# Moving the S1, S2 and S3 visits of an FFT filter and maxout kernel to other steps

## The chip, the cores and the metric

The kernel runs on one core of a Trainium2 chip. The metric is the time of one execution in microseconds (us) on the device, the median of several runs. The profile is of one execution of its own.

## The reference

The input x has 8 batches of 3072 positions with 256 channels. Each batch is filtered in the frequency domain, and each token of the result goes through a maxout layer:

```python
X = np.fft.rfft(x, axis=1)
y = np.fft.irfft(X * (filt_r + 1j * filt_i)[None], n=3072, axis=1)
t = y.reshape(8 * 3072, 256)
out = np.maximum(t @ w1, t @ w2) @ w_out          # w1, w2: 256 x 1024, w_out: 1024 x 256
```

The kernel uses max(a, b) = b + relu(a - b): it multiplies by Wd = w1 - w2, clips at zero, multiplies by w_out, and adds t @ M with M = w2 @ w_out.

## The kernel before

**The filter.** The transform of length 3072 is split into 96 by 32, so that each piece is a matrix product. For one batch there are these pieces:

- `load_xf` (SyncE's DMA queue) and `fold` (GpSimd) bring in x in 8 chunks and form, for each chunk, the sum (line 103) and the difference (104) of the two halves of the sequence. The result is a tile xb.
- `s1(b, c)`, one for each chunk c of 0 to 7: four TensorE matmuls with CT into two PSUM tiles pa (line 349), two ScalarE evictions to at (353), and for odd c two DMAs to DRAM (ad). `s1_read` reads ad back, transposed, as bt.
- `s2(b, n)`, n of 0 to 5: eight matmuls of bt into two tiles px (376). `product` multiplies each px by the filter F on VectorE (382), giving pq.
- `s3(b, n)`: sixteen matmuls of pq into two tiles pz (399), two ScalarE evictions to zt (403), a DMA to DRAM (zd). `z_read` reads zd back as zr, in two halves.
- `s4(tt)`: eight matmuls of zr into two tiles py (428); one is evicted by ScalarE (432), one by VectorE (434). This gives y for a block tt of 384 tokens, eight blocks to a batch.

**The maxout layer.** `moe_h(tt, j)`, j of 0 to 7, multiplies y by 128 columns of Wd into a tile ph (448) and evicts it with relu to gt, on ScalarE (452) or on VectorE (450). From block 8 on, the steps with j of 1, 3 and 6 go to VectorE; before that, `on_v` lists them. `moe_o(tt, ...)` accumulates gt and y into a tile po (478, 480); each full po is copied to ot by VectorE (492), and `out_block` sends ot off by DMAs that GpSimd issues (461).

**The order.** All engines run their instructions in the order in which the program issues them, which is written out by hand. A batch b has 64 steps (step = 8 i + j, for block tt = 8 b + i). Each step issues `moe_h` of this block, then the visits planned for the step, then three or four matmuls of `moe_o` of the block before, then other planned work (`todo`: loads, folds, reads, t2). At j = 4 (at j = 6 in a batch's last block), s4 of the next block ends the step:

```python
for j in range(8):
    step = 8 * i + j
    if tt < 8 * B:
        moe_h(tt, j)
    for fn, a in mid.get((b, step), ()):       # visits
        fn(*a)
    ... # moe_o(tt - 1, ...)
    for fn, a in todo.get((b, step), ()):
        fn(*a)
    if j == (4 if i < 7 else 6) and tt + 1 < 8 * B:
        s4(tt + 1)
```

A visit works on the next batch and on the one after: `visit(b + 1, n, quads)` issues s3 of the visit before (n of 1 to 6), s2 of this one (n of 0 to 5), s1 of batch b + 2 for the chunks in `quads`, and the two products. Seven visits make a batch. `plan_f2(b, steps, quads, xs, folds)` gives their steps, the chunks of each, the steps of the loads (xs) and those of the folds. It also plans `z_read` three steps after the fourth and the seventh visit, and `s1_read` six steps after the last (eleven in batch 0). Batch 6 has no s1 left to do, and batch 7 has no visits.

**PSUM.** pa, px, pz, py, ph and a few others share one pool, `ps`, of six buffers; po has two buffers of its own. A new tile takes the buffer that has been free for longest in the program's order, and its first matmul waits for the eviction that frees it.

**The start.** Batch 0's filter runs by another path, with everything on chip: `t2(c, engines)` transposes chunk c of zT into PSUM (553) and copies it to zr, on VectorE (556), on ScalarE (558), or half on each. GpSimd forms Wd (292) and casts w2 (285) for `prep_t`, which transposes it (299).

Of the kernel before, what the change touches and what calls it, by code (L numbers as in the profile page):

```python
# [26 lines left out]
def kernel(  # L27
# [15 lines left out]
    V, S, G, TE = nc.vector, nc.scalar, nc.gpsimd, nc.tensor  # L43
# [621 lines left out]
    def plan(b, step, fn, *a):  # L665
        todo.setdefault((b + step // 64, step % 64), []).append((fn, a))

    def plan_f1(b, nb, steps, read):
        for c, n in zip(range(4, 16), steps):
            plan(b, n, f1, nb, c, S if c % 2 == 0 else V)  # L670
        plan(b, read, f1_read, nb)
# [3 lines left out]
    def plan_f2(b, steps, quads, xs, folds):  # L675
        for n, st in enumerate(steps):
            mid.setdefault((b, st), []).append((visit, (b + 1, n, quads[n])))
        plan(b, steps[3] + 3, z_read, b + 1, 0)
        plan(b, steps[6] + 3, z_read, b + 1, 1)
        if b + 2 < B:  # L680
            for c in range(8):
                plan(b, xs[c], load_xf, b + 2, c)
                plan(b, folds[c], fold, b + 2, c)
            plan(b, steps[-1] + (6 if b else 11), s1_read, b + 2)

    plan(0, 2, t2, 1, (V,))
    plan(0, 7, prep_t, 0)
    plan(0, 8, prep_t, 1)
    plan(0, 9, prep_m)
    for c in range(2, 8):  # L690
        plan(0, 8 * (c - 2) + (7 if c == 2 else 8), t2, c, (V,))
    plan_f1(0, 1, (5, 6, 7, 7, 10, 10, 11, 11, 12, 12, 13, 13), 14)
    plan_f2(0, (25, 28, 31, 35, 38, 42, 46), ((0,), (1,), (2,), (3,), (4,), (5,), (6, 7)),
            (8, 10, 15, 18, 21, 27, 30, 33), (16, 19, 25, 28, 31, 34, 38, 42))
    for b in range(1, B - 1):
        plan_f2(b, (7, 14, 18, 24, 31, 38, 42) if b > 1 else (14, 18, 24, 30, 34, 39, 42), ((0, 1), (2,), (3,), (4,), (5,), (6,), (7,)),
                range(-32, 32, 8) if b > 1 else range(-25, 31, 7), range(-22, 42, 8) if b > 1 else range(-15, 41, 7))

    for tt in range(8 * B + 1):
        b, i = divmod(tt, 8)  # L700
# [45 lines left out]
```

## Time and profile before

| | us |
|---|---|
| median of 3 runs (502.82 to 503.9) | 503.05 |
| profiled execution | 502.04 |
| its span, first to last instruction | 500.2 |
| TensorE busy | 488.7 (98%) |
| VectorE busy | 331.4 (66%) |
| ScalarE busy | 308.6 (62%) |
| GpSimd busy | 259.7 (52%) |

PE is TensorE's matmuls, PEld its weight loads, DVE VectorE, ACT ScalarE, POOL GpSimd, SP SyncE. The mean granted clock of TensorE is 0.992 of full speed. A line of the timeline gives the start, the length from first start to last end, the engine, the line of the kernel, the operation, its tiles and how many were merged. Matmuls are pipelined, so lines of TensorE overlap, and the time that one group takes is read from its start to the start of the next. Idle time of an engine and what ended it stand in brackets.

### The profile page before, as it was taken

What the parts mean: (1) busy time and instruction counts of PE and PEld (TensorE: products, weight loads), DVE (VectorE), ACT (ScalarE), POOL (GpSimd) and SP (SyncE); (2) the same over time, 40 slices, a digit from 0 to 9 for tenths busy, and PEclk for the clock granted to TensorE, in tenths of its full rate; (3) what the DMA queues carried; (4) which work ended last, traced back from release to release, by engine and by line L of the source; (5) the groups of instructions that cost most, each with busy time, mean ns of one, the idle gap of its engine ahead of it and who ended that gap; (6) DMA issues with size and microseconds to landing.
All of it is one profiled execution on the core that took longest, in us unless ns stands there. A gap on an engine that the chain in (4) does not pass through costs nothing.

```text
span 500.2 us, 13079 instructions
## 1 busy us (share of the span) xinstructions
PE 488.7 (98%) x5300; PEld 361.7 (72%) x5300; DVE 331.4 (66%) x514; ACT 308.6 (62%) x629; POOL 259.7 (52%) x342
## 2 busy tenths in 40 slices
PE   8699999999999999999999999999999999999996
PEld 4456767777777777777777777777777777777775
DVE  7786788458865786567755787457764687555552
ACT  6777478657764777557674677547774565544442
POOL 7894678548463954627654764637632221222220
PEclk9979999999999999999999999999999999999999
DMA  7999889996899668978789568896759236411112
GB/s 122 166 245 210 260 218 272 294 257 208 234 285 244 180 206 236 240 186 235 206 236 282 178 182 250 222 234 202 201 185 249 84 113 144 167 65 64 64 64 84
DMA packets 77981, 97.19 MB, mean 194 GB/s; under 512 B 8033, under 2 KB 54370, under 8 KB 77858
## 3 DMA queue, kind: packets, MB, share of 16 engines
q1 hardware_dynamic: 64658, 66.73, 51.4%
q0 software_dynamic: 13264, 29.64, 20.5%
q8 instruction: 41, 0.67, 0.6%
q14 instruction: 18, 0.15, 0.1%
HBM read 53.87 MB, written 47.19 MB: 202 GB/s over the span
## 4 chain that ended last, share of the span: by engine, by line
PE 93%; ACT 2%; DMA 1%; DVE 1%; POOL 1%; issue 0%; POOLq 0%
PE po L480 34%; PE ph L448 33%; PE po L478 8%; PE pz L399 5%; PE py L428 4%; PE pa L349 2%; PE px L376 2%; DMA xb<-in_x_dram 1%; PE pt L532 1%; PE pr L553 1%; PE pt L526 1%; PE pa L324 1%; ACT at L509 1%; DVE pq L382 0%; ACT bt L518 0%
## 5 line engine op out<-in xcount | busy, mean ns | idle before, releaser
L480 PE MATMUL po<-Wo,gt 128*128 128x256 bf16 x1536 | 261.0, 273 | 0.0
L452 ACT ACTIVATE gt<-ph 128x384 bf16<-128x384 f32 x321 | 157.2, 496 | 144.9 <-PE ph L448 144.2
L480 PEld LDWEIGHTS <-gt 128*128 128x128 bf16 x1536 | 146.6, 98 | 66.0 <-issue 10.3
L461 POOL DMA_DIRECT2D out_dram<-ot x186 | 103.0, 557 | 171.5 <-DVE ot L492 168.9
L450 DVE TENSOR_SCALAR gt<-ph 128x384 bf16<-128x384 f32 x191 | 105.0, 554 | 64.0 <-PE ph L448 62.0
L382 DVE TENSOR_TENSOR pq<-px,F 128x1024 bf16<-128x1024 f32 x91 | 107.0, 1220 | 23.3 <-PE px L376 22.7
L448 PEld LDWEIGHTS <-Wd 128*128 128x128 bf16 x1024 | 96.5, 98 | 12.1 <-issue 0.5
L103 POOL TENSOR_TENSOR xb<-XF 128x512 bf16<-128x512 f32 x48 | 61.3, 1276 | 53.1 <-PE py L428 24.3
L492 DVE COPY ot<-po 128x512 f32<-128x512 f32 x95 | 65.2, 686 | 25.1 <-PE po L480 24.0
L104 POOL TENSOR_TENSOR xb<-XF 128x512 bf16<-128x512 f32 x48 | 61.1, 1273 | 0.0
L353 ACT ACTIVATE at<-pa 128x512 bf16<-128x512 f32 x96 | 51.8, 608 | 2.4 <-PE pa L349 2.1
L403 ACT ACTIVATE zt<-pz 128x512 bf16<-128x512 f32 x84 | 45.6, 594 | 11.8 <-PE pz L399 9.7
L428 PE MATMUL py<-G,zr 96*128 96x96 bf16 x512 | 32.7, 206 | 0.4 <-DVE zr L556 0.3
L428 PEld LDWEIGHTS <-zr 96*128 96x128 bf16 x512 | 28.9, 97 | 3.0 <-DVE zr L556 1.0
L399 PE MATMUL pz<-pq,VP 64*64 64x256 bf16 x336 | 22.2, 281 | 0.1
L376 PE MATMUL px<-bt,U 64*64 64x256 bf16 x384 | 20.2, 277 | 1.2 <-ACT VQ L273 0.7
L399 PE MATMUL pz<-pq,VQ 64*64 64x256 bf16 x336 | 21.0, 269 | 0.0
L399 PEld LDWEIGHTS <-VP 64*64 64x64 bf16 x336 | 9.8, 105 | 13.6 <-issue 13.3
L349 PE MATMUL pa<-xb,CT 64*64 64x512 bf16 x192 | 19.5, 383 | 0.0
L376 PEld LDWEIGHTS <-U 64*64 64x64 bf16 x384 | 10.5, 108 | 4.1 <-issue 3.8
L563 PE MATMUL pd<-W 128*128 128x512 bf16 x28 | 10.2, 488 | 1.5 <-DVE zero L145 1.5
L349 PEld LDWEIGHTS <-CT 64*64 64x64 bf16 x192 | 8.7, 105 | 2.1 <-ACT gt L452 1.2
(429 smaller groups left out, 606.3 us busy)
## 6 DMA issues: line engine op xcount, KB each, us to landing
out_dram<-ot POOLq DMA_DIRECT2D x186, 128.0 KB, 3.5
XF<-in_x_dram SPq DMA_DIRECT2D x96, 192.0 KB, 5.1
ad<-at SPq DMA_DIRECT2D x56, 192.0 KB, 3.7
zd<-zt SPq DMA_DIRECT2D x42, 256.0 KB, 2.6
zr<-zd SPq DMA_DIRECT2D x56, 192.0 KB, 5.0
bt<-ad SPq DMA_DIRECT2D x13, 768.0 KB, 9.8
WS<-in_moe_w_dram SPq DMA_DIRECT2D x4, 512.0 KB, 7.1
xb<-in_x_dram POOLq DMA_DIRECT2D x8, 192.0 KB, 5.9
```

What stands on the lines that cost most here:

```text
L103: G.tensor_tensor(t_[:, 0], f[:, 0], f[:, 1], OP.add)
L104: G.tensor_tensor(t_[:, 1], f[:, 0], f[:, 1], OP.subtract)
L353: S.activation(at[:, m0:m0 + 2], pa[g], AF.Copy)
L382: E.tensor_tensor(pq, px.rearrange("p (o i) d -> p o i d", o=1).to_broadcast([128, 2, 2, D]), F[:, :, 2 * v:2 * v + 2, s], OP.mult)
L399: TE.matmul(pz[g][64 * s:64 * s + 64, i], tab[64 * g:64 * g + 64, 2 * v + i, s], pq[s][64 * g:64 * g + 64, q, i], start=(q == 0), stop=(q ...
L428: TE.matmul(py[:, m], zr[b][:, 4 * i + m, 128 * dc:128 * dc + 128], G1, start=True, stop=True)
L448: TE.matmul(ph, Wd[:, dc, 128 * j:128 * j + 128], y_[:, dc], start=(dc == 0), stop=(dc == 1))
L450: V.tensor_scalar(gt[tt][:, j], ph, 0.0, None, OP.max)
L452: S.activation(gt[tt][:, j], ph, AF.Relu)
L461: E.dma_start(out=dst, in_=ot[tt // 2][:, 3 * (tt % 2) + c])
L480: TE.matmul(p_, g_[:, n - 2, blk], Wo[:, n - 2], start=(e == 0), stop=(e == 9))
L492: V.tensor_copy(ot[tt // 2][:, e - 1:e + 1], po[q // 2 % 2])
```

## The change

Steps and chunks are planned anew; the work itself is the same, except that one t2 is split between two engines.

- t2 of chunk 1, at step 2 of batch 0, goes half to ScalarE and half to VectorE.
- Batch 0's second and third visits move from steps 28 and 31 to 29 and 32.
- In batches 1 to 5 the first visit has one s1 chunk instead of two, and the last has two instead of one.
- In batches 2 to 6 the visits move from steps 7, 14, 18, 24, 31, 38, 42 to 7, 12, 18, 23, 28, 34, 39; in batch 1 from 14, 18, 24, 30, 34, 39, 42 to 14, 18, 23, 28, 34, 39, 42. The steps of loads and folds stay, those of `z_read` and `s1_read` move with the visits.

```diff
-    plan(0, 2, t2, 1, (V,))
+    plan(0, 2, t2, 1, (S, V))
...
-    plan_f2(0, (25, 28, 31, 35, 38, 42, 46), ((0,), (1,), (2,), (3,), (4,), (5,), (6, 7)),
+    plan_f2(0, (25, 29, 32, 35, 38, 42, 46), ((0,), (1,), (2,), (3,), (4,), (5,), (6, 7)),
             (8, 10, 15, 18, 21, 27, 30, 33), (16, 19, 25, 28, 31, 34, 38, 42))
     for b in range(1, B - 1):
-        plan_f2(b, (7, 14, 18, 24, 31, 38, 42) if b > 1 else (14, 18, 24, 30, 34, 39, 42), ((0, 1), (2,), (3,), (4,), (5,), (6,), (7,)),
+        plan_f2(b, (7, 12, 18, 23, 28, 34, 39) if b > 1 else (14, 18, 23, 28, 34, 39, 42),
+                ((0,), (1,), (2,), (3,), (4,), (5,), (6, 7)),
                 range(-32, 32, 8) if b > 1 else range(-25, 31, 7), range(-22, 42, 8) if b > 1 else range(-15, 41, 7))
```

## The prediction

> **What bounds the kernel now.** I read the page first. TensorE carries the chain, with almost nothing between its instructions.
>
> ```profile
> PE 488.7 (98%) x5300; PEld 361.7 (72%) x5300; DVE 331.4 (66%) x514; ACT 308.6 (62%) x629; POOL 259.7 (52%) x342
> PE 93%; ACT 2%; DMA 1%; DVE 1%; POOL 1%; issue 0%; POOLq 0%
> ```
>
> Then I cut the span into batches (table of windows: us, then busy us of each engine): TensorE is busy for the whole of a steady batch, so a moved visit costs or gains only what it makes TensorE wait.
>
> ```profile
> 222.49:279.90 57.41, 57.41 (x612) 42.92 (x608) 38.37 (x56) 37.06 (x77) 34.27 (x42) 1.00 0.81 221
> ```
>
> The page's waits are too coarse for this, so I read TensorE's timeline from start to start. A step is .65 to .76 us, or 1.10 with an s4. A visit adds 1.09: .09 for the turn to 64-row tiles, s3 .46, s2 .22, one s1 .32. A second s1 in the same visit adds .22 (the first line below, the last visit of batch 0, has 86.72 to 87.26 = .54 for two). Whatever exceeds that is waiting. The third line is a clean s4: py to the next ph in .34.
>
> ```profile
> 86.72 0.60 PE L349 MATMUL pa<-xb,CT 64*64 64x512 bf16 x8
> 222.32 0.81 PE L349 MATMUL pa<-xb,CT 64*64 64x512 bf16 x8
> 227.10 0.51 PE L428 MATMUL py<-G,zr 96*128 96x96 bf16 x8
> 227.44 0.49 PE L448 MATMUL ph<-y__4206,Wd 128*128 128x384 bf16 x2
> ```
>
> **What the change removes.** The pa of a visit's last s1 takes the PSUM buffer of the same step's ph, so it waits for that ph's eviction. An eviction on VectorE takes 558 ns against ScalarE's 491, and the pa comes at about the moment when the latter ends.
> - Batches 2 to 5: step 7 has .75 for its two s1 (222.32 to 223.07) against .54: .21. Steps 14 and 38 (VectorE): .38 against .32 each: .06. Step 24, the first of a token block, whose ScalarE eviction has one more semaphore to pass: .05. New steps 7 (one s1 and no s3, so no buffer of its own step), 12, 18, 23, 28, 34, 39 are all ScalarE steps: 0, as at 18 and 31 now. Gain .38 a batch, 1.54 in four.
> - Batch 1: step 14 .28 (.82 for two s1), 24 .05, 30 .06: .39. Batch 6 has no s1: nothing.
> - Batch 0: step 28 runs from 64.20 to 67.32, 3.12 us, and step 29 ends at 68.08. Moved: step 28 in 1.10, step 29 with the visit 1.86 (as 132.22 to 134.08), and .06, since its ph is on VectorE: end at 67.22. Gain .86; step 32, where the next visit now shares VectorE with t2, may give .1 of it back, or none.
> - t2 split over ScalarE and VectorE: py waits for zr until 40.10. The halves have rows (.59 on ScalarE, .42 on VectorE, in t2 of chunk 0), so zr is ready some .28 earlier. But step 7's pt starts at 41.91 behind GpSimd's cast of w2b, whose first half ends at 41.85 and does not depend on py. I take 0; the ends are -.28 and +.1 (ScalarE's next evictions .1 late).
>
> **What it adds at steps 12 and 28.** There j = 4, and an s4 follows in the same step. In the built order py takes the two buffers that zt0 and zt1 release, and the next ph the one that at0 releases: three evictions in a row on ScalarE. Batch 0's step 28 is such a visit today (first five lines TensorE, then ScalarE):
>
> ```profile
> 65.39 0.48 PE L376 MATMUL px<-bt,U 64*64 64x256 bf16 x8
> 65.61 0.48 PE L349 MATMUL pa<-xb,CT 64*64 64x512 bf16 x4
> 66.03 0.61 PE L480 MATMUL po<-Wo,gt 128*128 128x256 bf16 x4
> 66.47 0.69 PE L428 MATMUL py<-G,zr 96*128 96x96 bf16 x8
> 67.32 0.48 PE L448 MATMUL ph<-y__1318,Wd 128*128 128x384 bf16 x2 [0.16 <-ACT at L353]
> 65.70 1.08 ACT L403 ACTIVATE zt<-pz 128x512 bf16<-128x512 f32 x2 [0.48 <-PE pz L399]
> 66.67 1.09 ACT L353 ACTIVATE at<-pa 128x512 bf16<-128x512 f32 x2
> ```
>
> py to ph is .85 instead of .34: .51 lost. ScalarE was idle before zt, so nothing of its load explains it; at0 ends 1.57 after zt begins, while TensorE would want the buffer 1.1 after that. In a steady visit zt begins .21 after px (229.30 against 229.09), at0 ends 1.79 after px, ph starts at 1.84, and the clean sum is .22 + .32 + .44 + .34 = 1.31: .52 again. Bounds 0 and .61 (with the .10 that this pa waited); I take .52. Visits with an s1 at such a step: one in batch 1 (28), two in each of batches 2 to 5, so 9 x .52 = 4.7. In batch 6, without s1, ph takes zt0's buffer, free by then: 0. Queued behind: y on ScalarE and VectorE, needed four steps later; no cost.
>
> **What it adds at step 39.** The s1 of chunk 7 moves there from step 42, while its fold stays planned at step 34, and a visit now stands at step 34. Its two products go into VectorE's queue ahead of that step's copy of ot, the two output DMAs on GpSimd wait for the copy, and the fold stands behind them in GpSimd's queue. Today batches 2 to 5 have no visit at 34: step 34 starts at 248.10, the second half of the fold ends at 253.46, 5.36 later, and s1 comes at 256.36. Batch 1 has the visit at 34 today and shows the new order (step 34 starts at 132.22; VectorE, then GpSimd):
>
> ```profile
> 133.53 2.36 DVE L382 TENSOR_TENSOR pq<-px,F 128x1024 bf16<-128x1024 f32 x2 [0.93 <-PE px L376]
> 135.80 0.68 DVE L492 COPY ot<-po 128x512 f32<-128x512 f32 x1
> 136.78 1.09 POOL L461 DMA_DIRECT2D out_dram<-ot  x2 [6.65 <-DVE ot L492]
> 137.89 1.28 POOL L103 TENSOR_TENSOR xb<-XF 128x512 bf16<-128x512 f32 x1
> 139.12 1.29 POOL L104 TENSOR_TENSOR xb<-XF 128x512 bf16<-128x512 f32 x1
> 137.36 0.49 PE L448 MATMUL ph<-y__2587,Wd 128*128 128x384 bf16 x2
> ```
>
> The fold ends at 140.41, 8.19 after step 34 began. The last line is step 39, 5.14 after step 34. In the changed visit the second s1 comes .88 (ph, s3) and .22 (first s1) later: 6.24. TensorE, in order, waits until about 8.24: 2.0 in each of batches 2 to 5, 8.0 together. Bounds 0 (the fold as early as today, 5.36) and 2.3 (GpSimd a slot later). I take 2.0, since every term is a row of the same order. Batch 1 keeps its chunk 7 at step 42, where the fold ends 1.15 before (140.41 against 141.55): no wait.
>
> The DMAs that move along: z_read of batches 2 to 5 from steps 27 and 45 to 31 and 42, s1_read from 48 to 45, on SyncE past loads of x at other steps. Four z_read issues hold SyncE 1.98 us in batch 0; the loads behind them feed folds that are used 5 to 20 us later; 0, or a few tenths if I am wrong.
>
> **Sum**, against the profiled execution (502.04; its span 500.2): -1.54 - .39 - .86 + 4.7 + 8.0 = +9.9, so 511.9. The median of the runs is 503.05, 1.01 above the profiled one: 513.0.
>
> **Rivals.**
> - Fold in time: the copy of ot or the fold comes as early as today, and only s4 loses. For it: VectorE has idle time around. Against it: the built order has both products before the copy, as batch 1 has. +1.9: 505.0. Chance .07.
> - No s4 loss, but the fold waits: if py and ph found other buffers. Against it: the built order names zt0, zt1, at0. +5.2: 508.3. Chance .06.
> - Faster: a visit's backlog delays nothing behind it. ScalarE's four evictions (2.17 us) and VectorE's two products (2.36 us) would have to clear at the pace of the steps without a visit; it decides at .5 us (at0 before 1.31 after px) and at 2.0 us (fold). Then only the gains are left, -2.8: 500.3. The one sight of each order speaks against it. Chance .05.
> - The clock falls. From 20.9 to 24.3 TensorE was busy for 1.14 of 3.4 us, and in the next 6.8 us the granted clock was half:
>
> ```profile
> 20.90:24.30 3.40, 1.14 (x40) 0.66 (x40) 2.85 (x4) 2.74 (x6) 3.33 (x4) 0.99 0.73 133
> 24.30:31.10 6.80, 6.21 (x132) 3.14 (x131) 6.65 (x6) 4.73 (x11) 6.80 (x4) 0.50 0.97 250
> ```
>
>   A wait of 2.0 us, with one pa inside it, leaves some 1.6 busy of 3.4; from 17.5 to 20.9 it was 2.51 and the clock stayed full. So the case lies between the two. Each spell would cost 6.8 x .5 = 3.4: 516.4 with one, 526.6 with four. Chance .10. The Trainium skill ("TensorE: Matmul & The Clock Gate", Part 1: The HAM clock gate) asks for an idle window of about 3.4 us before the clock is halved. By that rule, which the row above does not bear out in full (a third of its window was busy), no spell comes, and the sum stays.
>
> **Numbers.** The forecast has .72. Its own range is 510 to 514.5. For 8 in 10 I reach from the 508.3 case to one spell of the slow clock: 508.0 to 517.0, which leaves out 500.3, 505.0 and several spells. A measurement here tells about 0.2% (1 us) from no change. Faster .05 (backlog rival), same .02 (a share of the fold rival in which s4 loses less), slower .93.
>
> **What would show it.** Right: four waits of TensorE at pa behind L103 and L104, each about 2 us in all, once per batch 2 to 5, with the fold ending some 8.2 after step 34; py to ph at .86 in nine visits; single pa at .32 and step 7 without a wait; pt still at 41.9. Wrong: no wait of TensorE on GpSimd; steady batches near 57.4; or a granted clock under 1.00 behind the waits.

## The result, and the profile after

The changed kernel takes 513.95 us (median of 6 runs, 513.49 to 515.13), the one before 502.94 (6 runs, 502.19 to 503.9): a ratio of 1.0223, 95% interval 1.0206 to 1.0239. The forecast was 513.0. The profiled execution took 513.72 with a span of 511.7, against 502.04 and 500.2: 11.5 us more span.

The page first: TensorE is 2.5 us busier in a span that is 11.5 longer (the same matmuls: part of a matmul's wait is counted as busy, 58.22 us in a steady batch against 57.41), and its share of the chain has fallen from 93% to 84%, with DMA, ScalarE and GpSimd on the chain.

```profile
PE 491.2 (96%) x5300; PEld 362.0 (71%) x5300; DVE 329.2 (64%) x514; ACT 308.8 (60%) x630; POOL 259.9 (51%) x342
PE 84%; DMA 5%; ACT 4%; POOL 4%; DVE 1%; issue 1%; POOLq 0%
```

The table of windows, from the start of a batch to the start of the next (batches 2 and 3, then batch 1, then batch 6): us, then TensorE's busy time. A steady batch takes 60.03 instead of 57.41, and no longer all of it is busy. Batch 1 takes 57.97; in the trace of before, its window 101.24 to 158.69 has 57.45. Batch 6, without s1, takes 55.29 as before (55.30).

```profile
159.84:219.87 60.03, 58.22 (x611) 43.17 (x608) 38.03 (x57) 37.12 (x77) 33.12 (x40) 1.00 0.81 217
219.87:279.90 60.03, 58.22 (x610) 43.16 (x608) 38.03 (x57) 37.13 (x77) 33.09 (x40) 1.00 0.77 212
101.87:159.84 57.97, 57.78 (x611) 42.99 (x608) 38.15 (x57) 36.92 (x77) 32.53 (x39) 1.00 0.91 243
399.97:455.26 55.29, 55.29 (x579) 41.54 (x576) 38.02 (x57) 29.55 (x61) 13.10 (x25) 1.00 0.36 116
```

So batches 2 to 5 cost 4 x 2.62 = 10.5 and batch 1 .52. What is left, .5, lies at the two ends: batch 1 starts .63 later (101.87 against 101.24), and what follows the last batch's matmuls is .15 shorter. The waits of TensorE alone (us in total, times, longest) name the new causes; of these five, the trace of before has only the third, once (.2 us, at batch 0's step 28):

```profile
PE pa L349 <- POOL xb L104: 3.4, 4, 0.8
PE pa L349 <- POOL xb L103: 2.4, 4, 0.6
PE ph L448 <- ACT at L353: 1.4, 9, 0.2
PE po L480 <- DMA Wo<-in_moe_w_out_dram: 0.8, 1, 0.8
PE ph L448 <- DVE pq L382: 0.6, 1, 0.6
```

The idle times are shorter than what is lost, because the modelled end of the matmul before covers the first part of each wait. From start to start the loss is whole. Step 39 of batch 3, on TensorE:

```profile
257.50 0.49 PE L448 MATMUL ph<-y__4679,Wd 128*128 128x384 bf16 x2
258.38 0.39 PE L349 MATMUL pa<-xb,CT 64*64 64x512 bf16 x4
259.35 0.37 PE L349 MATMUL pa<-xb,CT 64*64 64x512 bf16 x1 [0.59 <-POOL xb L103]
260.57 0.41 PE L349 MATMUL pa<-xb,CT 64*64 64x512 bf16 x3 [0.84 <-POOL xb L104]
260.91 0.50 PE L480 MATMUL po<-Wo,gt 128*128 128x256 bf16 x3
```

The two s1 take 258.38 to 260.91 = 2.53 instead of .54: 1.99 lost. VectorE and GpSimd show why, in the order that batch 1 had shown before: the visit's products, the copy of ot, the two output DMAs, the fold.

```profile
253.67 2.36 DVE L382 TENSOR_TENSOR pq<-px,F 128x1024 bf16<-128x1024 f32 x2 [0.93 <-PE px L376]
255.94 0.68 DVE L492 COPY ot<-po 128x512 f32<-128x512 f32 x1
256.92 1.09 POOL L461 DMA_DIRECT2D out_dram<-ot  x2 [4.83 <-DVE ot L492]
258.02 1.28 POOL L103 TENSOR_TENSOR xb<-XF 128x512 bf16<-128x512 f32 x1
259.24 1.27 POOL L104 TENSOR_TENSOR xb<-XF 128x512 bf16<-128x512 f32 x1
```

Step 34 starts at 252.35, so the fold ends 8.16 after it. And step 28 of batch 3, with s4 behind the visit (TensorE, then ScalarE): py to ph is 248.66 - 247.80 = .86 instead of .34, while pa takes a clean .31.

```profile
247.04 0.39 PE L349 MATMUL pa<-xb,CT 64*64 64x512 bf16 x4
247.80 0.70 PE L428 MATMUL py<-G,zr 96*128 96x96 bf16 x8
248.66 0.32 PE L448 MATMUL ph<-y__4498,Wd 128*128 128x384 bf16 x1 [0.16 <-ACT at L353]
247.03 1.09 ACT L403 ACTIVATE zt<-pz 128x512 bf16<-128x512 f32 x2
248.00 1.09 ACT L353 ACTIVATE at<-pa 128x512 bf16<-128x512 f32 x2
```

### The profile page after: what moved, and what is told of

The parts are those of the page before. It is cut to its first block, busy times and chain, and to the rows that moved or that the text cites. A ratio compares the mean times of both kernels' runs of the same rounds, so it can differ in the third digit from the quotient of the medians.

```text
span 511.7 us, 13077 instructions
## 1 busy us (share of the span) xinstructions
PE 491.2 (96%) x5300; PEld 362.0 (71%) x5300; DVE 329.2 (64%) x514; ACT 308.8 (60%) x630; POOL 259.9 (51%) x342
## 4 chain that ended last, share of the span: by engine, by line
PE 84%; DMA 5%; ACT 4%; POOL 4%; DVE 1%; issue 1%; POOLq 0%
PE po L480 31%; PE ph L448 31%; PE po L478 8%; PE pz L399 4%; PE py L428 3%; DMA Wo<-in_moe_w_out_dram 2%; ACT zt L403 2%; PE px L376 2%; PE pa L349 2%; DMA xb<-in_x_dram 1%; DMA zd<-zt 1%; DVE pq L382 1%; POOL xb L103 1%; POOL xb L104 1%; ACT at L353 1%
## 5 line engine op out<-in xcount | busy, mean ns | idle before, releaser
L480 PE MATMUL po<-Wo,gt 128*128 128x256 bf16 x1536 | 261.1, 273 | 0.8 <-DMA Wo<-in_moe_w_out_dram 0.8
L480 PEld LDWEIGHTS <-gt 128*128 128x128 bf16 x1536 | 146.2, 98 | 67.5 <-issue 12.4
L450 DVE TENSOR_SCALAR gt<-ph 128x384 bf16<-128x384 f32 x191 | 104.5, 553 | 70.9 <-PE ph L448 59.3
L492 DVE COPY ot<-po 128x512 f32<-128x512 f32 x95 | 65.2, 686 | 37.9 <-PE po L480 35.0
L428 PE MATMUL py<-G,zr 96*128 96x96 bf16 x512 | 34.1, 205 | 0.4
L349 PE MATMUL pa<-xb,CT 64*64 64x512 bf16 x192 | 20.4, 378 | 5.7 <-POOL xb L104 3.4
L349 PEld LDWEIGHTS <-CT 64*64 64x64 bf16 x192 | 8.7, 105 | 8.7 <-issue 4.4
## 6 DMA issues: line engine op xcount, KB each, us to landing
bt<-ad SPq DMA_DIRECT2D x13, 768.0 KB, 10.5
```

The lines of the kernel that those rows point to most:

```text
L428: TE.matmul(py[:, m], zr[b][:, 4 * i + m, 128 * dc:128 * dc + 128], G1, start=True, stop=True)
L450: V.tensor_scalar(gt[tt][:, j], ph, 0.0, None, OP.max)
L480: TE.matmul(p_, g_[:, n - 2, blk], Wo[:, n - 2], start=(e == 0), stop=(e == 9))
L492: V.tensor_copy(ot[tt // 2][:, e - 1:e + 1], po[q // 2 % 2])
```

## The experiments

The theory: two losses that have nothing to do with each other, the fold of chunk 7 behind step 34's visit (8.0) and s4 behind a visit (9 x .52), against gains of some 2. The rivals: the fold is late for its load, steps at j = 4 are dear by themselves, or the two s1 of the last visit are. The runs were made on three chips, and each is compared with the kernel before on its own chip, where that took 502.93 or 503.79 us. In the cuts of code, ... stands for what is left out of a line.

**The fold a step earlier.**

```diff
-    ... range(-22, 42, 8) if b > 1 else range(-15, 41, 7))
+    ... (-22, -14, -6, 2, 10, 18, 26, 33) if b > 1 else range(-15, 41, 7))
```

> The changed kernel with the fold of chunk 7 planned at step 33 instead of 34 in batches 2 to 6, so that GpSimd has it ahead of the output DMAs that wait for step 34's copy of ot. Theory (the fold stands in GpSimd's queue behind a copy that stands behind the visit's two products): the wait of 1.99 us at step 39 goes in all four batches, 513.95 - 4 x 1.99 = 506.0, and the s4 losses of .515 stay. Rival (the load of x or SyncE's order makes the fold late): the fold ends as late as before, 513.5 to 514.5. Rival (the clock or the rest gives part back): between.

506.54 us, 1.0060 of the kernel before (1.0037 to 1.0083), where the changed kernel had 1.0223. The fold now ends at 253.65, 3.8 us before the visit's s1 begins, ahead of the outputs in GpSimd's queue, and the two s1 of step 39 take .54:

```profile
252.38 1.27 POOL L104 TENSOR_TENSOR xb<-XF 128x512 bf16<-128x512 f32 x1
255.99 1.12 POOL L461 DMA_DIRECT2D out_dram<-ot  x2 [2.33 <-DVE ot L492]
257.44 0.60 PE L349 MATMUL pa<-xb,CT 64*64 64x512 bf16 x8
257.98 0.50 PE L480 MATMUL po<-Wo,gt 128*128 128x256 bf16 x3
```

The load was there in time, then; the place in the queue was the cause. The nine losses at py stay at .515 each.

**The user of the fold a visit later.**

```diff
-    ... (7, 12, 18, 23, 28, 34, 39) if b > 1 else (14, 18, 23, 28, 34, 39, 42), ...
+    ... (7, 12, 18, 23, 28, 34, 42) if b > 1 else (14, 18, 23, 28, 34, 39, 42), ...
```

> The changed kernel with the last visit of batches 2 to 6 at step 42 instead of 39; the fold of chunk 7 stays at step 34, behind the visit of that step. Theory: the fold ends as late as in the changed kernel, about 8.2 after step 34 begins, but s1 of chunk 7 comes about 2.2 later and finds it done or nearly done: -8.0 + 0 to .4, 506.0 to 506.5. Rival (two s1 in the last visit, not the fold, make the wait): it stays, 513 to 514.

506.42 us, 1.0072 (1.0053 to 1.0091). Step 34 starts at 250.26 and the fold ends as late as in the changed kernel, but the last visit's two s1, from 258.46 on, need no wait:

```profile
255.92 1.28 POOL L103 TENSOR_TENSOR xb<-XF 128x512 bf16<-128x512 f32 x1
257.15 1.27 POOL L104 TENSOR_TENSOR xb<-XF 128x512 bf16<-128x512 f32 x1
258.46 0.60 PE L349 MATMUL pa<-xb,CT 64*64 64x512 bf16 x8
```

So a late fold costs nothing by itself, and two s1 in one visit do not make the wait either. They are not quite free: py to ph takes .42 instead of .34 at step 44 of these four batches, as in the run with the chunks alone below.

**The visits off the steps with s4.**

```diff
-    ... (7, 12, 18, 23, 28, 34, 39) if b > 1 else (14, 18, 23, 28, 34, 39, 42), ...
+    ... (7, 13, 18, 23, 29, 34, 39) if b > 1 else (14, 18, 23, 29, 34, 39, 42), ...
```

> The changed kernel with the visits of steps 12 and 28 one step later, at 13 and 29 (j = 5, also a ScalarE step), ahead of which s4 has been issued. Theory (py and the next ph wait for the zt and at evictions of the visit just before): nine times .515 go, 513.95 - 4.6 = 509.3, the waits at step 39 stay. Rival (ScalarE is simply too full around j = 4 and 5, wherever the visit stands): most of the .515 stays and shows up at the next ph or pa, 513 to 514.

510.01 us, 1.0119 (1.0095 to 1.0144). In its trace all nine py are clean, and the visits at 13 and 29 have no wait. The waits at step 39 are 1.99 to 2.00, as before.

**One such visit on the kernel before.**

```diff
-    ... (7, 14, 18, 24, 31, 38, 42) if b > 1 else (14, 18, 24, 30, 34, 39, 42), ...
+    ... (7, 12, 18, 24, 31, 38, 42) if b > 1 else (14, 18, 24, 30, 34, 39, 42), ...
```

> The kernel before with one edit: the second visit of batches 2 to 6 at step 12 instead of 14. Step 12 is a ScalarE step with an s4 behind the visit. Theory: in each of batches 2 to 5 it loses .515 at py and the next ph and gains the .06 that step 14 waits now, so 4 x .455 = +1.8: 504.8 against 502.94; batch 6 shows neither. Rival (the change's own idea, a ScalarE step is better): 4 x -.06, 502.7.

505.19 us against 502.93: 1.0049 (1.0030 to 1.0068), 1.5 to 3.4 us more, with 1.8 expected. Step 12 loses .515 in batches 2 to 5 and nothing in batch 6. Its lines in batch 3: .86 from py to ph.

```profile
229.07 0.70 PE L428 MATMUL py<-G,zr 96*128 96x96 bf16 x8
229.93 0.48 PE L448 MATMUL ph<-y__4206,Wd 128*128 128x384 bf16 x2 [0.16 <-ACT at L353]
```

**s4 a step later, the visits left.**

```diff
-            if j == (4 if i < 7 else 6) and tt + 1 < 8 * B:
+            if j == (5 if i < 7 else 6) and tt + 1 < 8 * B:
```

> The changed kernel with s4 issued at the end of the step j = 5 instead of j = 4 in all blocks but a batch's last; the visits stay at 12 and 28. Theory (buffers): between visit and s4 one step of .76 us passes, so that the evictions are over, and py takes buffers that are free: 9 x .515 less, 509.3. Rival (a visit at j = 4 is dear by itself): 513 to 514.

512.27 us, 1.0171 (1.0151 to 1.0192): 1.7 us less than the changed kernel, where 4.6 were expected. The loss at py is gone (172.38 to 172.72 is a clean .34), so the nearness of visit and s4 is what costs. A new wait has come three steps on: the first ph of the next block needs VectorE's half of y, and that eviction now stands behind the visit's products and a copy of ot. In batch 2 (TensorE, then VectorE):

```profile
172.38 0.51 PE L428 MATMUL py<-G,zr 96*128 96x96 bf16 x8
172.72 0.49 PE L448 MATMUL ph<-y__3214,Wd 128*128 128x384 bf16 x2
174.14 0.72 PE L448 MATMUL ph<-y__3375,Wd 128*128 128x384 bf16 x2
171.07 2.36 DVE L382 TENSOR_TENSOR pq<-px,F 128x1024 bf16<-128x1024 f32 x2 [0.81 <-PE px L376]
173.34 0.68 DVE L492 COPY ot<-po 128x512 f32<-128x512 f32 x1
173.94 0.55 DVE L434 TENSOR_SCALAR y__3375<-py 128x384 bf16<-128x384 f32 x1
```

y ends at 174.49 and ph, begun at 174.14, takes .56 instead of .33. The loss is .24 in the nine visits that had .515, and .45 in the two of batch 6, which had none, so the trace gains 9 x .28 - .9 = 1.6 in batches 1 to 6. The expectation had looked at buffers alone.

**Both repairs.** The fold at step 33 and the visits at 13 and 29.

```diff
-    ... (7, 12, 18, 23, 28, 34, 39) if b > 1 else (14, 18, 23, 28, 34, 39, 42), ...
+    ... (7, 13, 18, 23, 29, 34, 39) if b > 1 else (14, 18, 23, 29, 34, 39, 42), ...
-    ... range(-22, 42, 8) if b > 1 else range(-15, 41, 7))
+    ... (-22, -14, -6, 2, 10, 18, 26, 33) if b > 1 else range(-15, 41, 7))
```

> Both edits on the changed kernel: fold of chunk 7 at step 33, visits at 13 and 29. Theory: the two losses are separate, so both go, 513.95 - 8.0 - 4.6 = 501.3, that is 1.6 below the kernel before. Rival (one of them hides part of the other): 502 to 504.

500.99 us against 503.79 on the same chip: .9949 (.9932 to .9966), faster than the kernel before by 1.7 to 3.4 us. A steady batch takes 57.06 and TensorE is busy for all of it:

```profile
212.85:269.91 57.06, 57.06 (x610) 42.88 (x608) 38.01 (x57) 37.33 (x76) 33.10 (x40) 1.00 0.78 222
```

57.41 - 57.06 = .35 is the gain of the change's own idea, which the two losses had covered; .38 a batch had been forecast, and step 39 now loses .05 at po.

**Batch 0's visits alone, on the kernel before.**

```diff
-    plan_f2(0, (25, 28, 31, 35, 38, 42, 46), ...
+    plan_f2(0, (25, 29, 32, 35, 38, 42, 46), ...
```

> The kernel before with batch 0's second and third visits at steps 29 and 32. The prediction's step: -.86, 502.1. What the changed kernel's trace suggests: of that, .2 goes at pa of step 29 and .74 at step 42, where the next ph has got the buffer of px and waits for VectorE's product: net -.1 to +.1, 502.9. If the wait at step 42 isn't there, it was not of this edit.

503.06 us against 502.93, ratio 1.0011 (.9988 to 1.0034): no gain. The pa of step 29 loses .20, and behind the visit of step 42 the next ph starts .74 late: in the built order it has px's buffer, and product 0 (VectorE, second line) frees that only at 84.4.

```profile
83.54 0.38 PE L478 MATMUL po<-M,y__1441 128*128 128x256 bf16 x2
83.21 2.35 DVE L382 TENSOR_TENSOR pq<-px,F 128x1024 bf16<-128x1024 f32 x2 [0.47 <-PE px L376]
84.48 0.48 PE L448 MATMUL ph<-y__1683,Wd 128*128 128x384 bf16 x2 [0.56 <-DVE pq L382]
```

**And the three later visits a step on.** Steps 38, 42 and 46 become 39, 43 and 47; the expectation calls them two.

```diff
-    plan_f2(0, (25, 28, 31, 35, 38, 42, 46), ...
+    plan_f2(0, (25, 29, 32, 35, 39, 43, 47), ...
```

> The kernel before with batch 0's visits at 25, 29, 32, 35, 39, 43, 47: as the second and third visit alone, but the two later ones a step on, where the built order gives the ph behind the sixth visit the buffer of zt, not that of px. Theory: the .74 wait is gone, and of the .86 some .6 are left: 502.3. Rival (the wait comes from late DMAs of zt): it stays, 502.9.

502.37 us, .9984 (.9961 to 1.0007): the time can't tell. In the trace the .74 is gone (.05 at each of the three visits moved on); the .20 at step 29 stays, and .13 at step 32.

**The chunks alone, on the kernel before.**

```diff
-    ... ((0, 1), (2,), (3,), (4,), (5,), (6,), (7,)),
+    ... ((0,), (1,), (2,), (3,), (4,), (5,), (6, 7)),
```

> The kernel before with only the chunks moved: the first visit of batches 1 to 5 has one s1, the last (step 42) two. Theory: step 7's wait of .21 goes in four batches and step 14's .28 in batch 1, but in batch 1 the second s1 of step 42 waits for the VectorE eviction of step 41 behind step 39's products (.40, as in the changed kernel): -.84 - .28 + .40 = -.72, 502.2. Rival (batches 2 to 5 show that wait at step 42 too): 503 to 504.

502.39 us, .9988 (.9973 to 1.0004): inconclusive in time. The trace has the .21 of step 7 gone in four batches and .28 in batch 1, .40 more at batch 1's step 42, and .08 at the py of step 44 in batches 2 to 5: -.84 - .28 + .40 + .33 = -.4.

**The split t2 alone, on the kernel before.**

```diff
-    plan(0, 2, t2, 1, (V,))
+    plan(0, 2, t2, 1, (S, V))
```

> The kernel before with only the t2 of chunk 1 split over ScalarE and VectorE; one look. Theory: zr is ready some .3 earlier and py with it, but TensorE then waits for GpSimd (Wd, cast of w2), so the fourth batch-0 transposes of w2 start when they did; 502 to 503.5, no change that the time can tell. Rival: the .28 stay.

502.58 us in a single run, which says nothing of so small a term. py starts earlier, as meant, and then ph waits for the last quarter of Wd and pt for w2 (TensorE, then GpSimd):

```profile
39.44 0.58 PE L428 MATMUL py<-G,zr 96*128 96x96 bf16 x8
41.38 0.50 PE L448 MATMUL ph<-y__990,Wd 128*128 128x384 bf16 x2 [0.82 <-ACT at L329]
42.35 0.62 PE L299 MATMUL pt<-I,w2b 128*128 128x128 bf16 x8
40.04 1.28 POOL L292 TENSOR_TENSOR Wd<-WS 128x512 bf16<-128x512 f32 x1
41.26 2.02 POOL L285 CAST w2b<-WS 128x1024 bf16<-128x1024 f32 x2
```

The profile puts the .82 down to ScalarE; but Wd ends at 41.32, and ph, which the program has wait for it, starts at 41.38.

**All of it.** Both repairs, and in the first two batches, on the changed kernel:

```diff
-    plan_f2(0, (25, 29, 32, 35, 38, 42, 46), ...
+    plan_f2(0, (25, 29, 32, 35, 39, 43, 47), ...
-    ... (7, 12, 18, 23, 28, 34, 39) if b > 1 else (14, 18, 23, 28, 34, 39, 42), ...
+    ... (7, 13, 18, 23, 29, 34, 39) if b > 1 else (13, 18, 23, 29, 34, 39, 45), ...
-    ... range(-22, 42, 8) if b > 1 else range(-15, 41, 7))
+    ... (-22, -14, -6, 2, 10, 18, 26, 33) if b > 1 else range(-15, 41, 7))
```

> Both repairs (fold of chunk 7 at step 33, visits at 13 and 29) and two more on the changed kernel: batch 0's visits at 25, 29, 32, 35, 39, 43, 47, and batch 1's at 13, 18, 23, 29, 34, 39, 45. Theory: from 501.0 (both repairs alone) the .74 of batch 0's step 42 and the .40 of batch 1's step 42 go as well, 499.9, .6% below the kernel before. Rival (new waits at the new steps): 500.5 to 502.

501.35 us, .9980 (.9956 to 1.0005): not shown to be better than the two repairs. The .74 and the .40 are gone, but batch 0's last visit at 47 puts off `s1_read` by a step, batch 1's first visit at 13 comes a step earlier, and its px waits .82 for bt (in the run with batch 0's three later visits a step on, which has the same `s1_read` and the visit at 14, it does not wait). Batch 2's first visit, behind a later `s1_read` too, loses .24 at its px and pa.

```profile
113.03 0.41 PE L376 MATMUL px<-bt,U 64*64 64x256 bf16 x7 [0.60 <-DMA bt<-ad]
```

## Why the prediction was right, and where its terms were off

- **Wait at step 39: right in place, cause and size.** 2.0 forecast, 1.99 measured, in four batches; the fold ends 8.16 after step 34 (8.19 forecast). The run with the earlier fold shows that GpSimd's queue was the cause, the one with the later visit that only its meeting with s1 costs. Batch 1, which had the order already, was the whole of the evidence.
- **s4 behind a visit: right.** .52 forecast, .515 measured, nine times, and nothing in batch 6. Moving the visit or s4 takes the loss at py away; putting one visit there brings it.
- **The steady gains: right.** .38 forecast; from start to start steps 7, 12, 18, 23, 28, 34 have a clean pa, and a batch costs 2.62 where 2.66 was forecast (2.0 + 1.04 - .38).
- **Batch 1: off by .40.** "Gain .39" against .515 lost at step 28 made +.13; measured +.52. The step that failed is the list of buffers: I took only a visit with an own-step buffer on a VectorE step to wait. At step 42 the second s1's pa takes the buffer of step 41's ph, a VectorE step, and that eviction stands behind step 39's products and a copy of ot: it ends at 142.63, and the last pa starts at 142.68. The two s1 take .93 there, 142.09 to 143.02 (TensorE, then VectorE). The run with the chunks alone has the same .94.

  ```profile
  142.09 1.00 PE L349 MATMUL pa<-xb,CT 64*64 64x512 bf16 x8
  143.02 0.39 PE L480 MATMUL po<-Wo,gt 128*128 128x256 bf16 x2
  141.48 0.68 DVE L492 COPY ot<-po 128x512 f32<-128x512 f32 x1
  142.08 0.55 DVE L450 TENSOR_SCALAR gt<-ph 128x384 bf16<-128x384 f32 x1
  ```

- **Batch 0: mis-sized, gain .86 forecast, none measured.** .20 goes at step 29, where I had .06: VectorE's y and the eviction behind it come later than I put them. .74 goes at step 42, for which I had no term: there the next ph waits for product 0 of the visit, that is, for the buffer of px. In the run with batch 0's visits alone the same two waits stand, and the time does not move.
- **t2: 0 forecast, and right**, though the first wait that eats the gain is for Wd, ahead of the cast of w2 that I named. The pt starts at 41.52, not at 41.9 as the prediction's sign had it: it stands .06 behind the first half of the cast in both traces, and GpSimd began that .39 earlier in this execution (40.41 against 40.80).
- **Not of the change: .58 ahead of step 16.** The first po waits for Wo's load: .97 from start to start, with TensorE .39 ahead by then. That load landed between 7.8 and 10.6 us after its issue across the profiles here, also in runs without the split t2, and TensorE waited for 0 to .97. What makes it vary stays open. So I take the profiled execution's +11.5 for some .6 too dear, and the medians' +11.0 for the better figure of the change: 10.5 + .5 of batches 1 to 5, and next to nothing of batch 0.
- **The clock rival did not come.** TensorE was busy for 2.12 of 3.55 us about the wait, and the granted clock (the 1.00) stayed:

```profile
257.70:261.25 3.55, 2.12 (x30) 1.09 (x29) 0.31 (x1) 2.80 (x6) 2.80 (x3) 1.00 0.64 231
```

  The rule of the Trainium skill ("TensorE: Matmul & The Clock Gate", Part 1: The HAM clock gate), that an idle window of some 3.4 us is needed, had said so, and the trace agrees here: the wait is 2.0 us, with a pa inside it. The start of the kernel before, with 1.14 busy of 3.4 and the clock halved after it, still shows that a window need not be wholly idle: its longest idle stretch was 1.54.
- **A step misread, without effect.** The first `z_read` of batches 2 to 5 moves from step 27 to 26, three steps after the fourth visit, not to 31 as the prediction has it; 31 is batch 1's. Every py in these batches that has no visit just ahead takes its clean .34, so no late zr shows.
- **The backlog rival and the fold rival** would have needed the evictions to keep their old pace; both traces have them in the order of the queue.

## What to carry to other kernels

When a block of work is moved to another step, list for each engine's queue what now stands behind it: here two VectorE products delayed a copy, the copy two DMA issues, these a fold that nobody had moved, and the fold the matmul that needs it, which now came earlier. If any other iteration of the loop already has the new order, its rows give the price before a run does. A change with one sound idea can lose by two places: repairing those two alone turned 2.2% slower into .5% faster.

## What was not expected of the hardware and the program

- Contrary to the section on the kernel before, the built order does not always hand out the one of the six PSUM buffers that has been released for longest in the program: behind the visit of batch 0's step 42 the next ph got px's buffer, not the one of zt, although zt was evicted on time. Why the build chose so was not settled; moving the visit by a step changed it.
- The load of Wo, issued at the same place of the program in each kernel, took 7.8 to 10.6 us to land. And where batch 0's third visit is at step 32, the fold of chunk 2 came late enough, behind a load of x, to hold it for .75, .31 and .13 in three of the runs; in the others the step loses .04 or .05. Ahead of batch 1 a single profile can't tell half a microsecond.
